# Sliding-window attention beside a SwiGLU: edge products on 64x32 and 32x64 tiles, V for sixteen heads, full products as column strips

## The chip, the core and the metric

The kernel runs on one core of one Trainium2 chip. The metric is the device time of one execution in microseconds, lower is better; the time before is the median of three runs, 240.3 us (240.14 to 240.38).

## What is computed

The input x has 2048 rows of 512. A 32-head attention (head size 16) with a causal window of 256 keys and a SwiGLU with 1376 hidden columns both read x; a sigmoid gate per row mixes their results.

```python
H = 32; Dh = D // H; W = 256
qkv = (x @ wqkv).reshape(B, S, 3, H, Dh)            # then q, k, v
scores = einsum("bhqd,bhkd->bhqk", q, k) * (Dh ** -0.5)
mask = (idx[:, None] - idx[None, :] >= 0) & (idx[:, None] - idx[None, :] < W)
p = softmax(where(mask, scores, -1e9))
a = (p @ v) @ wo
b = (silu(x @ w1) * (x @ w3)) @ w2
g = sigmoid((x * gate_w).sum(-1))
out = g * a + (1 - g) * b
```

Operands are bf16.

## The kernel before

**Tiles.** x is held transposed (xT, 512 channels in four chunks of 128 partitions, 2048 columns). The attention is done in four passes c = 0 to 3, each with the eight heads whose 128 channels fill the partitions: four row groups s of 32 partitions hold two heads each, a = 0 and 1. Keys are kept twice, once per head of the pair, with the other head's 16 partitions set to zero (`rowsA` is that 0/1 column), so that a score product of 32 rows serves one head. Queries stand in qT. The 2048 rows are 16 key tiles t of 128, or four stretches of 512 (tq for projections, h for edges, w for values).

**Scores.** `main_batch(c, t)` computes, for key tile t, the queries from 64 behind the tile's start, 256 of them (L560): eight matmuls of 32 rows x 128 columns, four row groups side by side, into the four banks of `su`. ScalarE takes the exponential of all of `su` at once (L564) into an Em buffer, and GpSimd cuts the two triangles outside the window (L569, L574). That leaves, for each key tile, two blocks of 64 x 64 in the window: the first 64 queries against the first 64 keys ("lo") and queries 320 to 383 against the last 64 keys ("hi"). `edge_batch(c, h)` makes these for four key tiles and both heads of each pair in one go (L610). Its stationary operand is 128 wide: 64 keys of one head and 64 of the other, side by side in `kz`; the result has one head's keys in partitions 0 to 63 and the other's in 64 to 127. The exponentials go to an Ee buffer (L614), masked by GpSimd (L627) and VectorE (L633, L637). The last key tile's queries 64 to 127 ride along in the last edge batch.

**Values.** `pv(c, w)` sums, for the 512 queries of stretch w, exponentials times V over the key tiles that reach them (L700). V has 16 columns per head and a column of ones (the softmax's denominator), so each matmul has 17 columns and is placed on one of four 32-column tiles; four heads stand side by side in a bank of `ch`, and the two heads of the pairs take two banks, jobs[0] and jobs[1]. For the edge blocks the stationary V has 128 rows, of which the other head's 64 are zero; these copies are made by GpSimd (L517) from the V that VectorE wrote (L512). VectorE then transposes, divides by the denominator and transposes back into OT (L724 to L734).

**The rest.** Projections of K and Q (L422), of V (L499, in pass 0 with the gate's weight as a 129th column), the up products (L825; the last 96 hidden columns are treated as 64 joint ones and 32 "tail columns", L785), the down products (L875), the output products (L905) with the mix and the DMA out (L909, L915). All of these are full products of 128 rows x 128 columns on TensorE.

**Order.** Nothing is looped at run time. Each piece is an `Op` with an engine, an assumed duration, a due time and buffers taken and freed; `Plan.emit` places the ops one by one on a list schedule and issues them in that order. The order on each engine is thus fixed when the program is built. `form` names an op's shape on TensorE ("full", "row", "column"); a change of form adds SWITCH to the plan, and `rank` groups ops of one form. The due times come from the numbers in K. `su` is one buffer of four banks, `ch` four buffers of one bank.

Of the kernel before, what the change touches and what calls it, by code (L numbers as in the profile page):

```python
# [26 lines left out]
class Op:  # L27
    __slots__ = ("eng", "dur", "lat", "fn", "deps", "due", "take", "free", "seq", "start", "end", "slots", "hold", "form")

    def __init__(self, eng, dur, fn, deps, due, take, free, lat, seq, form):  # L30
        self.eng, self.dur, self.fn, self.due, self.lat, self.seq = eng, dur, fn, due, lat, seq
        self.deps = [d for d in deps if d is not None]
        self.take, self.free = take, free
        self.start = self.end = None
        self.hold = 0.0
        self.form = form

# [8 lines left out]
class Plan:  # L46


    def __init__(self, slots, beside, apart):
        self.ops = []  # L50
        self.slots = slots
        self.beside, self.apart = beside, apart

# [16 lines left out]
    def rank(self, op, form):  # L70
        due = op.due
        if op.eng == "PE" and op.form != "full":
            if form != "full":
                due -= self.beside
            elif op.form == "column":
                due += self.apart
        return due, op.seq

    def emit(self):
# [15 lines left out]
        while ready:  # L95
# [23 lines left out]
            if eng == "PE" and op.form != form:  # L119
                est = max(est, engine.get(eng, 0.0) + SWITCH)  # L120
                form = op.form
# [20 lines left out]
        self.order = order  # L142
        for est, op in order:
            op.fn()
# [3 lines left out]
def kernel(  # L148
# [27 lines left out]
    NV = NT * 4  # L176
    LO, HI = NV, 2 * NV
    VW = DH + 1
    HALF = (0, 1, 2, 3, 4)
    SCALE = float(DH) ** -0.5  # L180
# [17 lines left out]
    wB = pp.tile([P, NDC, 2 * FB], BF16, name="wB")  # L198
# [3 lines left out]
    kz = pp.tile([P, NT, 4, KB], BF16, name="kz")  # L202
    qT = pp.tile([P, S + KB], BF16, name="qT")
    k1 = pp.tile([P, NT, 2, KB], BF16, name="k1")
    vs = pp.tile([P, 3 * NV, 2 * VW], BF16, name="vs")
    gwr = pp.tile([NDC, P], BF16, name="gwr")
    wv0 = pp.tile([P, NDC, P + 4], BF16, name="wv0")
# [8 lines left out]
    mlast = pp.tile([P, 2, KB], BF16, name="mlast")  # L216
    Em = [pp.tile([P, 4, 2, 256], BF16, name=f"Em_{i}") for i in range(9)]
    Ee = [pp.tile([P, 4, 4, 2, KB], BF16, name=f"Ee_{i}") for i in range(2)]
    kt = [pp.tile([P, 512], BF16, name=f"kt_{i}") for i in range(2)]
# [10 lines left out]
    K = {"T0": 6.663, "TA": 234.789, "TF0": -1.359, "TF1": 251.583, "PV": 0.213, "EDGE": -2.966, "HOLD": -4.301, "LEAD": 9.863, "QLEAD": -3.864, "V": 5.26, "O0": -0.819, "O1": 5.827, "O2": 6.852, "O3": 24.592, "FE": -3.084, "PE": -2.787, "VE": -3.291, "MK": 4.4, "UP": 2.598, "_km": 1.0, "_lo": 1.0, "LE": 4.467, "ADJ": 0.265, "SEP": 1.114, "BE": -2.825}  # L230
    plan = Plan({"su": 1, "ch": 4, "Em": len(Em), "Ee": len(Ee), "kt": 2, "tt": 2, "h1": 2,
# [3 lines left out]


    def half_of(base, a):
        return slice(0, KB) if (a == 1) == (base == LO) else slice(KB, P)
# [19 lines left out]
    def constants3():  # L258
        nc.gpsimd.memset(qT[:, S:S + KB], 0.0)
        for m in (medge, mlast):  # L260
            nc.gpsimd.memset(m[:], BIG)
        for m, k, sign, halves in ((medge, 0, 1, (0, KB)), (medge, 1, -1, (0, KB)),
                                   (mlast, 0, 1, (0, KB)), (mlast, 1, 1, (KB,))):
            for lo in halves:
                nc.gpsimd.affine_select(out=m[lo:lo + KB, k, :], in_=m[lo:lo + KB, k, :],
                                        pattern=[[sign, KB]], compare_op=ALU.is_ge, fill=0.0,
                                        base=0 if sign > 0 else -1, channel_multiplier=-sign)

    def constants4():
        nc.gpsimd.memset(hb[:], 0.0)  # L270
        nc.vector.memset(vs[:, LO:LO + NV, :], 0.0)
        nc.vector.memset(vs[:, HI:HI + NV, :], 0.0)
        nc.gpsimd.memset(vs[:, 0:NV, DH:2 * VW:VW], 1.0)
        for base in (LO, HI):
            for a in range(2):
                nc.gpsimd.memset(vs[half_of(base, a), base:base + NV, a * VW + DH], 1.0)

# [106 lines left out]
    def gw_out():  # L384
        nc.vector.tensor_copy(out=wv0[:, :, P:P + 1],
                              in_=ch[gjob.at["ch"]][:].bitcast(BF16)[:, 0:NDC].rearrange("p (c o) -> p c o", o=1))

    def wv0_copy():
        nc.vector.tensor_copy(out=wv0[:, :, 0:P], in_=wqkv_sb[:, :, 2 * D:2 * D + P])

    a = add("PE", 0.1, gw_turn, [gw_in], 9.407, take=[(gjob, "ch")])
    wv0_ready = [add("DVE", 0.15, gw_out, [a], 9.0, free=[(gjob, "ch")]),
                 add("DVE", 0.3, wv0_copy, [qkv_in[2]], 9.0)]
# [11 lines left out]
    def projections(c, tq):  # L405
# [3 lines left out]
        if c:  # L409
            war = [su_ops[(c - 1, t)] for t in range(4 * tq, 4 * tq + 4)]  # L410
            war.append(far_ops[(c - 1, tq)])
            vwar = [pv_ops[(c - 1, w)] for w in range(tq, min(NTC, tq + 2))]
            qwar = [su_ops[(c - 1, t)] for t in range(max(0, 4 * tq - 3), 4 * tq + 4)]
            qwar += [far_ops[(c - 1, h)] for h in range(max(0, tq - 1), tq + 1)]
        else:
            vwar, qwar = [], []
        src = list(xt_ready[tq]) + [qkv_in[2 if c < 2 else 3]]

        def chain(job, col, lo, hi, t0=0, t1=512):
            pst = ch[job.at["ch"]]  # L420
            for dc in range(lo, hi):
                nc.tensor.matmul(pst[:, t0:t1], lhsT=wqkv_sb[:, dc, col + c * P:col + (c + 1) * P],  # L422
# [10 lines left out]
        kv0 = kz[:, 4 * tq:4 * tq + 4, 1:3, :]  # L433
        kv1 = kz[:, 4 * tq:4 * tq + 4, 0:4:3, :]

        k1v = k1[:, 4 * tq:4 * tq + 4, :, :]

        def by_half(src):
            return src.rearrange("p (k h t) -> p k h t", h=2, t=KB)
        a = project(kj, D, [qkv_in[0 if c < 2 else 3]], due, [(kj, "ch")])  # L440
        if c == 0:
            def kev_a():
                nc.vector.tensor_scalar_mul(
                    out=kv0, in0=by_half(ch[kj.at["ch"]][:]),
                    scalar1=rowsA[:, 0:1])

            def kev_b():
                nc.scalar.activation(
                    out=k1v, in_=by_half(ch[kj.at["ch"]][:]),
                    func=ACT.Copy, scale=rowsA[:, 1:2])  # L450
            b = add("DVE", 0.69, kev_a, [a], due, free=[(kj, "ch")])
            def kev_c():
                nc.gpsimd.tensor_copy(out=kv1, in_=k1v)
            m = add("ACT", 0.69, kev_b, [b], due, free=[(kj, "ch")])
            k_ready[(c, tq)] = [b, m]
            ke_ready[(c, tq)] = [add("POOL", 0.62, kev_c, [m], due)]
        else:
            def kev():
                nc.vector.tensor_copy(out=kt[kj.at["kt"]][:], in_=ch[kj.at["ch"]][:])

            def kcopy():
                (nc.vector if K["_km"] else nc.gpsimd).tensor_copy(out=kv1, in_=k1v)

            def kmask(h):
                (nc.vector if K["_km"] else nc.gpsimd).tensor_scalar_mul(  # L465
                    out=(kv0, kv1, k1v)[h], in0=by_half(kt[kj.at["kt"]][:]),
                    scalar1=rowsA[:, min(h, 1):min(h, 1) + 1])
            b = add("DVE", 0.69, kev, [a], due, take=[(kj, "kt")], free=[(kj, "ch")])
            k_ready[(c, tq)] = [add("DVE" if K["_km"] else "POOL", 0.3 if K["_km"] else 1.64, lambda h=h: kmask(h), [b] + war, due, free=[(kj, "kt")])
                                for h in (0, 2)]  # L470
            ke_ready[(c, tq)] = [add("DVE" if K["_km"] else "POOL", 0.3 if K["_km"] else 0.62, kcopy, k_ready[(c, tq)], due)]
# [12 lines left out]

        vdue = due + K["V"]
        res = []
        gates = []
        for m0, nm in ([(4 * tq, 2), (4 * tq + 2, 2)] if c == 0 else [(4 * tq, 4)]):
            vj = Job()
            w = P + 1 if c == 0 else P  # L490

            def vmm(lo, hi, vj=vj, m0=m0, w=w):
                pst = ch[vj.at["ch"]]
                for mm in range(lo, hi):
                    m = m0 + mm
                    for dc in range(NDC):
                        rhs = (wv0[:, dc, 0:w] if c == 0
                               else wqkv_sb[:, dc, 2 * D + c * P:2 * D + (c + 1) * P])
                        nc.tensor.matmul(pst[:, mm * w:(mm + 1) * w], lhsT=xT[:, dc, m * P:(m + 1) * P],  # L499
                                         rhs=rhs, start=(dc == 0), stop=(dc == NDC - 1))  # L500

            def v_of(rows, base, a, m0=m0, nm=nm):
                return vs[rows, base + 4 * m0:base + 4 * (m0 + nm), a * VW:a * VW + DH]

            def v_all(vj=vj, m0=m0, nm=nm, w=w):
                out = vs[:, 4 * m0:4 * (m0 + nm), :].rearrange("p i (a e) -> p i a e", a=2)[:, :, :, 0:DH]
                src = ch[vj.at["ch"]][:, 0:nm * w].rearrange("p (m w) -> p m w", w=w)[:, :, 0:P]
                src = src.rearrange("p m (s a d) -> p m s a d", s=4, a=2)
                out = out.rearrange("p (m s) a d -> p m s a d", s=4)
                for m in range(1 if w == P else nm):  # L510
                    n = nm if w == P else 1
                    nc.vector.tensor_copy(out=out[:, m:m + n], in_=src[:, m:m + n])  # L512

            def v_half(base, a, v_of=v_of):
                to = half_of(base, a)
                half = slice(0, KB) if base == LO else slice(KB, P)
                nc.gpsimd.tensor_copy(out=v_of(to, base, a), in_=v_of(half, 0, a))  # L517

            def zact(vj=vj, m0=m0, nm=nm, w=w):
                z = ch[vj.at["ch"]][:, 0:nm * w].rearrange("p (m w) -> p m w", w=w)  # L520
# [448 lines left out]
```

## Time and profile before

| | |
|---|---|
| median of three runs | 240.3 us |
| the profiled execution, its time / its span | 240.56 / 238.8 us |
| granted TensorE clock | 1.00 |
| first projection starts / last matmul ends | 5.84 / 235.7 us into the span |
| TensorE, mean duration of a 512-column full product (L825) | 380 ns, x320 |
| main scores (L560), 480 matmuls | 278 and 268 ns |
| edge scores (L610), 512 matmuls | 189 ns |
| value products reading Ee (L700), 992 matmuls | 193 ns |
| ScalarE, exponential of 128 x 2048 (L564, L614) | 1877 ns, x76 |
| GpSimd, V copies of L517 | 30.6 us busy in 80 |
| VectorE, V out of PSUM (L512) / key copies (L462) / last edge mask (L637) | 8.2 + 3.7 / 4.8 / 5.4 us busy |
| VectorE, mix and bank out (L909) | 737 ns, x15 |

Each figure is from one execution. "Busy" is the union of an engine's instructions. Matmuls overlap each other: a duration of 380 ns does not mean that the next one starts 380 ns later, so the timeline's start times say what one costs. In the timeline a row is a group of equal neighbours: start, time from the first start to the last end, engine, line, operation, out<-in, rows*columns of the stationary operand, moving operand, count. In the list of waits each row says who waited for whom, the total, how many times and the longest. In the list of stretches each engine's busy time stands with its count of instructions, in the order TensorE, its weight loads, VectorE, ScalarE, GpSimd.

### The profile page before, as it was taken

Reading aid. Unit: us, or ns where it says so; the run is one execution under the profiler, and the core shown is the slowest. Engines: PE = TensorE matmul, PEld = TensorE weight load, DVE = VectorE, ACT = ScalarE, POOL = GpSimd, SP = SyncE. Lnnn points to the kernel's source line nnn. Section 1 sums busy time; section 2 is a strip of 40 time slices with the busy share of each in tenths; the row PEclk is TensorE's granted clock in tenths of the full one; section 3 lists DMA queues with packets and bytes.
Section 4 is the critical chain, followed back from the end, with each engine's and each line's share of the span. In section 5 each row is a group of like instructions: output and inputs, shape, how many; then the busy total and the mean of one; then the engine's idle time right before and its main releaser. Section 6 shows DMA issues by size and latency. Waiting matters only on the chain.

```text
span 238.8 us, 8528 instructions
## 1 busy us (share of the span) xinstructions
PE 231.3 (97%) x3738; PEld 118.8 (50%) x3738; DVE 201.3 (84%) x342; ACT 171.2 (72%) x141; POOL 159.6 (67%) x261
## 2 busy tenths in 40 slices
PE   8999999999999999999989899999999999999994
PEld 8554544546463543545454544545454545445442
DVE  5576998967699989996699999987899897969885
ACT  3389798876867898666858788776768989766510
POOL 7259967979857877587475777768494968575500
PEclk9999999999999999999999999999999999999999
DMA  7999980000000000000000000000000001002133
GB/s 199 205 335 276 201 212 17 5 1 3 3 3 0 5 11 11 7 0 3 3 3 3 1 8 20 3 0 3 3 3 5 3 0 25 3 22 69 52 108 110
DMA packets 20413, 11.59 MB, mean 49 GB/s; under 512 B 9656, under 2 KB 20376, under 8 KB 20376
## 3 DMA queue, kind: packets, MB, share of 16 engines
q1 hardware_dynamic: 19680, 10.59, 17.7%
q8 instruction: 29, 0.48, 0.9%
q10 hardware_dynamic: 696, 0.46, 0.6%
q14 instruction: 8, 0.07, 0.1%
HBM read 6.85 MB, written 2.10 MB: 37 GB/s over the span
## 4 chain that ended last, share of the span: by engine, by line
PE 72%; DVE 19%; ACT 4%; issue 2%; POOL 1%; DVEq 0%; ACTq 0%
PE ch L825 20%; PE ch L875 15%; PE ch L422 9%; PE ch L700 8%; PE su L560 6%; PE ch L905 5%; PE ch L499 4%; ACT Ee L614 4%; DVE h L839 3%; PE su L610 2%; DVE Ee L633 2%; DVE hT L845 2%; DVE Ee L637 2%; DVE tn L724 2%; DVE k L465 2%
## 5 line engine op out<-in xcount | busy, mean ns | idle before, releaser
L564 ACT ACTIVATE Em<-su 128x2048 bf16<-128x2048 f32 x60 | 112.6, 1877 | 34.6 <-PE su L560 31.4
L825 PE MATMUL ch<-xT,w_sb 128*128 128x512 bf16 x320 | 79.3, 380 | 0.5 <-DVE vs L512 0.3
L569 POOL TENSOR_SCALAR_AFFINE_SELECT Em<-Em 64x512 bf16<-64x512 bf16 x60 | 41.1, 685 | 32.5 <-ACT Em L564 26.9
L627 POOL TENSOR_SCALAR_AFFINE_SELECT Ee<-Ee 64x1024 bf16<-64x1024 bf16 x32 | 42.7, 1333 | 21.4 <-ACT Ee L614 19.3
L825 PEld LDWEIGHTS <-w_sb 128*128 128x128 bf16 x320 | 28.4, 98 | 34.8 <-issue 6.9
L875 PE MATMUL ch<-w_sb,hT 128*128 128x512 bf16 x160 | 40.3, 380 | 0.0
L574 POOL TENSOR_SCALAR_AFFINE_SELECT Em<-Em 64x512 bf16<-64x512 bf16 x56 | 37.3, 665 | 3.2
L614 ACT ACTIVATE Ee<-su 128x2048 bf16<-128x2048 f32 x16 | 30.0, 1876 | 10.3 <-PE su L610 7.6
L422 PE MATMUL ch<-xT,wqkv_sb 128*128 128x512 bf16 (+1 forms) x136 | 34.3, 372 | 0.0
L517 POOL COPY vs<-vs 64x256 bf16<-64x256 bf16 (+1 forms) x80 | 30.6, 382 | 5.1 <-DVE vs L512 1.8
L839 DVE SCALAR_TENSOR_TENSOR h<-tt,ch 128x512 bf16<-128x512 bf16 (+1 forms) x44 | 29.6, 677 | 4.7 <-ACT tt L835 4.5
L845 DVE SCALAR_TENSOR_TENSOR hT<-h,ch 128x512 bf16<-128x512 bf16 x40 | 27.1, 677 | 1.9
L835 ACT ACTIVATE tt<-ch 128x512 bf16<-128x512 f32 (+1 forms) x44 | 25.7, 594 | 2.4 <-PE ch L825 2.2
L700 PEld LDWEIGHTS <-vs 128*17 128x17 bf16 x1664 | 21.1, 92 | 8.6 <-issue 6.3
L700 PE MATMUL ch<-Em,vs 128*17 128x256 bf16 (+2 forms) x672 | 22.9, 242 | 2.4 <-DVE h L839 1.7
L700 PE MATMUL ch<-Ee,vs 128*17 128x64 bf16 x992 | 22.6, 193 | 0.0
L875 PEld LDWEIGHTS <-hT 128*128 128x128 bf16 x160 | 13.9, 98 | 16.8 <-issue 3.2
L422 PEld LDWEIGHTS <-wqkv_sb 128*128 128x128 bf16 x136 | 12.4, 99 | 12.7 <-issue 2.1
L499 PEld LDWEIGHTS <-xT 128*128 128x128 bf16 x256 | 15.8, 97 | 5.6 <-issue 1.8
L880 DVE TENSOR_SCALAR bsb<-ch,omg 128x512 bf16<-128x512 f32 x15 | 11.2, 747 | 7.6 <-PE ch L875 7.4
L560 PE MATMUL su<-qT,kz 32*128 32x256 bf16 x240 | 17.3, 278 | 0.2
L560 PE MATMUL su<-qT,k 32*128 32x256 bf16 x240 | 16.7, 268 | 0.0
(81 smaller groups left out, 257.4 us busy)
## 6 DMA issues: line engine op xcount, KB each, us to landing
out_dram<-ot SPq DMA_DIRECT2D x15, 128.0 KB, 1.7
wqkv_sb<-in_A_wqkv_dram SPq DMA_DIRECT2D x5, 256.0 KB, 5.7
w_sb<-in_B_w_dram SPq DMA_DIRECT2D x1, 1280.0 KB, 6.7
w_sb<-in_B_w_dram SPq DMA_DIRECT2D x2, 608.0 KB, 7.8
w_sb<-in_B_w_dram SPq DMA_DIRECT2D x2, 512.0 KB, 5.2
w_sb<-in_B_w_dram SPq DMA_DIRECT2D x2, 256.0 KB, 4.9
wo_sb<-in_A_wo_dram SPq DMA_DIRECT2D x1, 512.0 KB, 5.5
xs<-in_A_x_dram SPq DMA_DIRECT2D x1, 256.0 KB, 2.9
```

The lines of the kernel that those rows point to most:

```text
L422: nc.tensor.matmul(pst[:, t0:t1], lhsT=wqkv_sb[:, dc, col + c * P:col + (c + 1) * P], rhs=xT[:, dc, tq * 512 + t0:tq * 512 + t1], start=(d ...
L560: nc.tensor.matmul(su[:, s, a * 256:(a + 1) * 256], lhsT=head_keys(r, t, a), rhs=qT[r, q0:q0 + 256], start=True, stop=True)
L564: nc.scalar.activation(out=Em[job.at["Em"]][:], in_=su[:].rearrange("p s (a q) -> p s a q", a=2), func=ACT.Exp, scale=SCALE)
L569: nc.gpsimd.affine_select(out=e, in_=e, pattern=[[0, 8], [1, KB]], compare_op=ALU.is_ge, fill=0.0, base=0, channel_multiplier=-1)
L574: nc.gpsimd.affine_select(out=e, in_=e, pattern=[[0, 8], [-1, KB]], compare_op=ALU.is_ge, fill=0.0, base=-1, channel_multiplier=1)
L614: nc.scalar.activation(out=Ee[ej.at["Ee"]][:].rearrange("p s t k q -> p s (t k q)"), in_=su[:], func=ACT.Exp, scale=SCALE)
L627: nc.gpsimd.affine_select(out=e, in_=e, pattern=[[0, 4], [0, 4], [1, KB]], compare_op=ALU.is_ge, fill=0.0, base=0, channel_multiplier=-1)
L700: nc.tensor.matmul(po[32 * s:32 * s + VW, lo - 512 * w:hi - 512 * w], lhsT=vs[:, i, a * VW:(a + 1) * VW], rhs=mov, start=(n == 0), stop=(n ...
L825: nc.tensor.matmul(ch[job.at["ch"]][:], lhsT=wA[:, dc, :] if joint else w[:, dc, f * P:(f + 1) * P], rhs=xT[:, dc, tcb * 512:(tcb + 1) * 512],
L839: nc.vector.scalar_tensor_tensor(out=h1[job.at["h1"]][ru, :], in0=tt[job.at["tt"]][rg, :], scalar=1.0, in1=ch[job.at["ch"]][rg, :], op0=AL ...
L845: nc.vector.scalar_tensor_tensor(out=dst, in0=h1[job.at["h1"]][ru, :], scalar=0.5, in1=ch[up.at["ch"]][ru, :], op0=ALU.mult, op1=ALU.mult)
L875: nc.tensor.matmul(bps[:], lhsT=ht[:, mm * P:(mm + 1) * P], rhs=w2_sb[0:fs, f, :], start=(f == 0), stop=(f == NFC - 1))
```

## The change

- **Edge scores** take keys of one head at a time: 64 keys as a 32 x 64 stationary operand, the two heads of a pair on the two 64-column halves. `kz` and `k1` become one `kh` (both heads, keys in order), so the copies between them go.
- **Value edges** take 64 rows: head a's keys are partitions 64a to 64a + 63 of Ee, and V's 64 rows come from `vs` itself or, where the other half of the tile's keys is meant, from `vx`, a copy of V with its halves exchanged (one GpSimd copy for each half of two key tiles). The zeroed copies of V go. In `pv` the main products of both heads come first, then one op of form "half" with all edge blocks, in which a and s run innermost.
- **The last key tile** gets its queries 64 to 127 from the score batch of tile 14: that batch's 256 columns are 192 of tile 14 and 64 of tile 15, as two matmuls for each head; a second GpSimd select cuts tile 15's triangle. `mlast` goes.
- **V** is projected for sixteen heads (256 columns) at once in passes 0 and 2, and serves two passes. The gate's column moves from V's product to that of the tail columns (65 instead of 64 columns).
- **Strips.** Full products go through `product`. Where an unbroken run of full and column ops on TensorE holds a column op, all full products of the run are written as four matmuls of 32 columns each. The plan no longer counts a change between "full" and "column".
- The numbers in K are others, so due times and with them the order on all engines differ.

```diff
+        run = []
+        for op in [op for est, op in order if op.eng == "PE"] + [None]:
+            if op and op.form in ("full", "column"):
+                run.append(op)
+                continue
+            column = any(o.form == "column" for o in run)
+            for o in run:
+                o.strips = column
+            run = []
         for est, op in order:
+            self.strips = op.strips
             op.fn()
...
+    def product(out, lhsT, rhs, start, stop):
+        if not plan.strips:
+            nc.tensor.matmul(out, lhsT=lhsT, rhs=rhs, start=start, stop=stop)
+            return
+        for j in range(0, P, 32):
+            nc.tensor.matmul(out[j:j + 32], lhsT=lhsT[:, j:j + 32], rhs=rhs, start=start, stop=stop)
...
+                        product(pst[:, mm * 256:(mm + 1) * 256], lhsT=xT[:, dc, m * P:(m + 1) * P],
+                                         rhs=wqkv_sb[:, dc, 2 * D + cp * 256:2 * D + cp * 256 + 256],
+                                         start=(dc == 0), stop=(dc == NDC - 1))
...
+            def vcross(a, m0=m0):
+                to, at_ = slice(KB * a, KB * a + KB), slice(KB - KB * a, P - KB * a)
+                nc.gpsimd.tensor_copy(out=vx[to, m0:m0 + 2, :, 0:DH], in_=vs[at_, cp, m0:m0 + 2, a:16:2, 0:DH])
...
-                    nc.tensor.matmul(su[:, s, a * 256:(a + 1) * 256], lhsT=head_keys(r, t, a),
-                                     rhs=qT[r, q0:q0 + 256], start=True, stop=True)
+                    n = min(256, S - q0)
+                    nc.tensor.matmul(su[:, s, a * 256:a * 256 + n], lhsT=kh[r, a, P * t:P * t + P],
+                                     rhs=qT[r, q0:q0 + n], start=True, stop=True)
+                    if t == NT - 2:
+                        nc.tensor.matmul(su[:, s, a * 256 + n:(a + 1) * 256], lhsT=kh[r, a, P * t + P:P * t + 2 * P],
+                                         rhs=qT[r, S - KB:S], start=True, stop=True)
...
+                    for a in range(2):
+                        for s in range(4):
+                            r = slice(32 * s, 32 * s + 32)
+                            if q0 < S:
+                                nc.tensor.matmul(su[KB * a:KB * a + KB, s, (2 * i + k) * KB:(2 * i + k + 1) * KB],
+                                                 lhsT=kh[r, a, k0:k0 + KB], rhs=qT[r, q0:q0 + KB],
+                                                 start=True, stop=True)
...
+        def edges(last):
+            for n, (t, q, k) in enumerate(lows + highs):
+                for a in range(2):
+                    rows = slice(KB * a, KB * a + KB)
+                    for s in range(4):
+                        values = (vs[rows, c // 2, t, 8 * (c % 2) + 2 * s + a, :] if a == k
+                                  else vx[rows, t, 4 * (c % 2) + s, :])
+                        value(a, s, values, Ee[ejob[(c, "e", t // 4)].at["Ee"]][rows, s, t % 4, k, :], q - q0,
+                                last and n == len(lows + highs) - 1)
...
         for a in range(2):
-            prev = add("PE", streams(0, cut), lambda a=a: mm(a, 0, cut), deps + [prev], due, take=[(jobs[a], "ch")], free=frees,
-                       form="column")
-            ends.append(prev)
+            prev = add("PE", streams(early), lambda a=a: mains(a, early), mdeps + [prev], due, take=[(jobs[a], "ch")],
+                       free=mfree, form="column")
+        prev = add("PE", 0.25, lambda: edges(not final), edeps + [prev], due,
+                   free=[(ejob[(c, "e", h)], "Ee") for h in range(max(0, w - 1), w + 1)], form="half")
```

More of the change, by code (lines that the diff above doesn't have):

```diff
@@ L473, in projections @@
+            k_ready[(c, tq)] = [add("DVE" if K["_km"] else "POOL", 0.3 if K["_km"] else 1.64, lambda h=h: kmask(h),
+                                    [b] + war, due, free=[(kj, "ot")]) for h in range(2)]
         qj = Job()
@@ L505, in v_all @@
[L505 to L512, printed above, removed]
@@ L704, in streams, with value @@
-        def streams(n0, n1):
-            return 0.035 + sum(hi - lo for kind, t, lo, hi in todo[n0:n1]) / 2400
-        cut = len(todo) - 1 if final else len(todo)
-        ends = []
+        begun = set()
+        def value(a, s, values, e, col, last):
+            first = (a, s) not in begun
+            begun.add((a, s))
+            nc.tensor.matmul(ch[jobs[a].at["ch"]][32 * s:32 * s + VW, col:col + e.shape[-1]], lhsT=values, rhs=e,
+                             start=first, stop=last, skip_group_check=True)
```

302 lines of the change are left out of this document (104 added, 198 removed).

## The prediction

> **What bounds the kernel now.** I read the busy shares first, then who TensorE waited for, then its instructions in order of time, and last groups by shape and busy time by stretch. The page's first line, and TensorE's waits:
>
> ```profile
> PE 231.3 (97%) x3738; PEld 118.8 (50%) x3738; DVE 201.3 (84%) x342; ACT 171.2 (72%) x141; POOL 159.6 (67%) x261
> ...
> PE ch L700 <- DVE h L839: 1.7, 2, 0.9
> PE su L296 <- DVE warm L299: 1.1, 1, 1.1
> PE ch L700 <- DVE hT L845: 0.5, 1, 0.5
> PE ch L825 <- DVE vs L512: 0.3, 1, 0.3
> ```
>
> TensorE is busy for 97% of the span and its waits come to some 4 us, mostly of value products (L700) for a bank that VectorE has not yet emptied. So TensorE's own work sets the time, and what a matmul costs is not its duration (they overlap) but the distance to the next start. The timeline gives these distances:
>
> ```profile
> 104.61 0.29 PE L560 MATMUL su<-qT,kz 32*128 32x256 bf16 x4
> 104.73 0.28 PE L560 MATMUL su<-qT,k 32*128 32x256 bf16 x4
> 104.94 1.04 PE L875 MATMUL ch<-w_sb,hT 128*128 128x512 bf16 x4
> 105.81 0.38 PE L875 MATMUL ch<-w_sb,hX 96*128 96x512 bf16 x1
> 106.03 1.06 PE L499 MATMUL ch<-wqkv_sb,xT 128*128 128x128 bf16 x16
> 106.93 0.59 PE L875 MATMUL ch<-w_sb,hT 128*128 128x512 bf16 x2
> ...
> 107.78 1.04 PE L875 MATMUL ch<-w_sb,hT 128*128 128x512 bf16 x4
> 108.75 0.21 PE L700 MATMUL ch<-Em,vs 128*17 128x64 bf16 x4
> ...
> 109.37 0.20 PE L700 MATMUL ch<-Em,vs 128*17 128x64 bf16 x4
> 109.40 0.20 PE L700 MATMUL ch<-Ee,vs 128*17 128x64 bf16 x4
> 109.43 0.20 PE L700 MATMUL ch<-Em,vs 128*17 128x64 bf16 x4
> ```
>
> A full product of 512 columns takes 0.217 us (104.94 to 105.81 for four), one of 128 takes 0.056 (106.03 to 106.93 for sixteen). Four value products on four 32-column tiles start within 0.01 us of each other and the next four follow after 0.03 us: 64 columns cost the same 0.029 us for four as for one. Four scores of 256 columns on four 32-row tiles take 0.11 to 0.12. A change of tile shape adds to that: 104.73 to 104.94 is 0.21 where the stream is 0.11, and 107.78 to 108.75 is 0.97 where four products are 0.87. I take 0.093 us, the middle of all such places in the trace (full to row 0.312 less 0.216, row to full 0.200 less 0.110, full to column 0.309 less 0.216).
>
> By these distances the order before holds 206.1 us of streams and 170 shape changes behind the opening, 15.8 us. The opening (first projection at 5.84) and 4.3 us of waits in 13 places bring that to 232.0 of the 235.7 us up to the last matmul's end; most of what is left is some 0.01 us that a first product after a wait or a change takes extra.
>
> **The change, part by part.** All counts are of instructions in the two programs' orders.
>
> *Value edges.* Before, 992 products of 64 columns read Ee (L700), four at a time: 248 x 0.029 = 7.2 us. After, 960 of 64 rows x 32 columns, ordered so that eight in a row lie on eight different tiles and two banks. If eight overlap as four do now, 120 x 0.029 = 3.5 us; if only four, 7.0. The trace holds no 64-row tile. I take the eight: L610 shows four row tiles side by side and L700 four column tiles, each starting 2 to 4 ns after the last, so eight need some 25 of the 29 ns. Another 32 products of 64 columns move to Em (key tile 15): 8 x 0.029 = 0.2. Sum -3.5 us (lower bound of the gain 0).
>
> *Edge scores.* 512 of 32 rows x 128 columns (128 groups x 0.029 = 3.7 us) become 960 of 32 x 64: 3.5 us with eight tiles, 7.0 with four. I take -0.2, worst +3.3.
>
> *Score tile 14.* Its eight 256-column scores become eight pairs, 192 columns and then 64 on the same row tile, pair by pair. All 3738 matmuls of the trace start in program order, and a second group on the same row tiles waits until the first has streamed (104.61 to 104.73). So each 64 waits for its 192 (0.083 us by 54 such groups of L700, 0.074 plus three starts) and the next pair waits behind it: 8 x 0.086 = 0.7 us, where eight scores took 0.22. Four such batches: +1.9 us. Were the pairs of other row tiles free to pass, it would be 0. I take the first, since nothing in the trace passes. The 32 edge scores that key tile 15 no longer needs are in the counts above. [...]
>
> *V.* 256 products of 128 or 129 columns (0.056 to 0.058: 14.4 us) become 128 of 256 (0.109, as L422's and L905's of that width): 14.0. -0.4 us. The gate's column moves to the tail columns: 64 products of 65 instead of 64 columns, 0.03 us. One shift in time: V now comes in c 0 and 2 alone.
>
> *Strips.* 596 instructions of 128 rows x 32 columns (532 of 512 columns, 64 of 256), four to a product, stand for 149 full products. Four 256-column value products on column tiles start 0.110 after the four before, against 0.109 for one full product, so a strip product costs what the full one does, +0.15 us for all. What strips buy are shape changes: written full, the new order would have 195, as it is 171, against 172 before. So strips only pay for the new shapes, and the sum of changes is -0.1 us. Bounds: 0 to, if strips overlapped badly, 0.01 a product more, 1.5 us.
>
> *Other engines.* VectorE loses L462 (4.8 us), L637 (5.4), the two memsets (1.9), 0.13 on each of twelve key masks (1.5) and 0.9 of V copies: some 14 of 201 us. GpSimd loses 30.6 us of L517 for 32 copies at 0.425 (13.6), and gains four selects at 0.69: -16 us net with L453. ScalarE loses four small tanh. None is on the path by itself; what they can move is TensorE's waits:
>
> ```profile
> 90.00:120.00 30.00, 29.45 (x490) 14.59 (x489) 25.61 (x41) 22.11 (x16) 19.96 (x29) 1.00 0.02 5
> 120.00:150.00 30.00, 28.24 (x507) 14.70 (x507) 29.08 (x45) 23.35 (x20) 21.24 (x31) 1.00 0.03 7
> ```
>
> The fourth figure behind the stretch is VectorE: 29.08 of 30 us in 120 to 150, the start of c = 2, where most of the waits are (0.96 us at 120, 0.83 at 135, 0.19 and 0.07 near 149). There V copies double (+2.7 us in that c) against -3.5 of other work, so I leave these waits. In c = 1 and 3 VectorE loses some 6 us each; the waits at 72 to 73 (0.55), 94 (0.62) and 184 (0.16) go: -1.2 us, bounds 0 and -4.3 (no wait left).
>
> *The end.* After the last value products TensorE had 8.8 us of output and up/down products, now 10.4; VectorE has five steps of the last normalisation and 13 evictions in it, at 0.62 from start to start 10.3 us. It keeps pace just about; the last eviction and its transfer (3.2 us behind the last matmul) stay.
>
> *Sum.* -3.5 - 0.2 + 1.9 - 0.4 + 0.2 - 0.1 - 1.2 = -3.3 us. The profiled execution took 240.56 us around its span of 238.8, the median of the runs is 240.3. 240.3 - 3.3 = **237.0 us**.
>
> **Rivals.**
>
> *Eight tiles do not overlap (12%, slower).* Value edges and edge scores each run four at a time. Price 3.5 + 3.5 us: 237.0 + 7.0 = 244.0 us; if only one of the two suffers, 240.5. For it: no such shape in the trace, and sixteen instructions would have to issue in 29 ns where eight do now. Against: bursts at the start of L610 and L700 issue one every 1.5 to 2 ns. It turns into a loss as soon as a group of eight takes over 0.043 us (3.3 / 240 more than 0.029).
>
> *Weight loads set the pace of small tiles (10%).* Four loads of 17 columns go by in 29 ns at L700. Were that their limit, an edge score group with two loads of 64 columns per row tile, 128 in place of 68, takes up to 0.055 us: 120 x 0.026 = 3.1 us more, 240.1 us, no change; strips, 128 columns in up to 0.055, stay hidden under 0.217. Against: the first group after a change is late by 0.006 us at 17 columns and by 0.010 with full loads, so loads look short and parallel. [...]
>
> *Tile 14's pairs pass each other (16%, faster).* Then 1.9 us less: 235.1 us.
>
> *VectorE falls behind at c = 2 (8%).* Twice the V copies meet the stretch that is 97% full. If its 2.7 us of extra copies all become waits of L700's banks, and the -1.2 of elsewhere stays: 239.7 us; if the -1.2 fails too, 240.9. Against: its total there falls. Half of this counts as faster, half as slower.
>
> **How the numbers follow.** Forecast 54%, pairs pass 16%, loads 10%, no overlap 12%, VectorE 8%. 0.2% is 0.5 us, about what a measurement can tell here: faster means below 239.8, slower above 240.8. Faster: 54 + 16 + 4 = 74%. Same: 8 of the loads' 10. Slower: 12 + 4 + 2 = 18%. Alone, the forecast has 235.5 to 238.5 (waits gone, strips 1.5 dearer). The range takes in the passing pairs with a microsecond of waits gone below, 234.0, and loads and VectorE above, 241.0; the 244 stays outside.
>
> **What would show it.** Groups of eight edge products starting 0.03 us apart (0.06 would be the first rival, 0.05 on the scores alone the second). Score tile 14 as a batch of 0.7 us. Strip products 0.22 us apart with no gap between strips and value products. About 171 gaps of 0.09. VectorE near 187 us, GpSimd near 144, TensorE waits near 3 us, most of them in c = 2. I am wrong if TensorE's waits grow past 6 us, or if its work shrinks by 4 or more or not at all.

## The result, and the profile after

The changed kernel takes 242.45 us (median of 6 runs, 241.72 to 243.25) where the kernel before takes 240.22 (6 runs on the same chip, 239.69 to 240.38): ratio 1.0095, 95% interval 1.0068 to 1.0122. It is slower by 2.2 us; 237.0 was forecast.

The profiled execution took 241.72 us around a span of 240.0; the one before had 240.56 around 238.8. So the two traces show 1.2 us of the 2.2. The rest lies in the spread of the changed kernel's runs (1.5 us, against 0.7), which no profile here explains.

The page's first line after, then the waits of TensorE, then busy time by stretch (columns as before):

```profile
PE 234.2 (98%) x4537; PEld 122.9 (51%) x4537; DVE 183.2 (76%) x311; ACT 171.1 (71%) x137; POOL 146.2 (61%) x205
```

```profile
PE su L301 <- DVE warm L304: 1.1, 1, 1.1
PE ch L606 <- issue: 0.5, 1, 0.5
PE ch L247 <- DVE h L781: 0.4, 1, 0.4
```

```profile
90.00:120.00 30.00, 30.00 (x680) 15.74 (x677) 22.93 (x37) 22.40 (x16) 19.70 (x27) 1.00 0.03 6
120.00:150.00 30.00, 29.87 (x567) 16.55 (x566) 26.25 (x48) 23.21 (x21) 19.99 (x28) 1.00 0.03 7
```

VectorE and GpSimd lost about what was forecast (183 and 146 us, where 187 and 144 were expected), and the waits behind the opening fell further than forecast, from 4.3 us to 1.4 (by the gaps between starts; the list leaves out the small ones). TensorE is busy for all of 90 to 120. Yet the last matmul starts at 236.02 us, where it started at 235.38. TensorE got *slower at its own work*, and a busy share can't show that. The timeline can. One window's value edges (start, time from the first start to the last end, and at the end of the row the count of products):

```profile
105.71 1.06 PE L606 MATMUL ch<-Em,vs 128*17 128x64 bf16 x48
...
106.70 0.20 PE L606 MATMUL ch<-Ee,vs 64*17 64x64 bf16 x4
106.71 0.20 PE L606 MATMUL ch<-Ee,vx 64*17 64x64 bf16 x4
...
106.80 0.33 PE L606 MATMUL ch<-Ee,vx 64*17 64x64 bf16 x8
106.95 0.22 PE L606 MATMUL ch<-Ee,vs 64*17 64x64 bf16 x4
106.99 0.22 PE L606 MATMUL ch<-Ee,vx 64*17 64x64 bf16 x4
107.02 0.22 PE L606 MATMUL ch<-Ee,vs 64*17 64x64 bf16 x4
...
107.15 0.22 PE L606 MATMUL ch<-Ee,vs 64*17 64x64 bf16 x4
107.30 0.29 PE L510 MATMUL su<-qT,kh 32*128 32x256 bf16 x4
```

At first four products start every 0.015 us, so eight in 0.03, as forecast: eight tiles do run side by side. The entry of eight products at 106.80 holds a pause; behind it four take 0.033 us, 8.3 ns for each product with its weight load. By the single starts, the pause comes behind the 32nd product, here and in each of the 32 batches of edge products (16 of values, 16 of scores); it is 99 to 108 ns long in 31 of them and 90 in one. A batch of 64 edge scores goes the same way: 32 in 0.139 us, a pause of 0.099, then 0.067 for each eight. It takes 0.497 us from first start to last, where the 32 products of 128 columns took 0.22 before. The granted clock is 1.00 in both kernels from 90 to 120 us, so the clock is not the cause.

The `issue` line in the list of waits is something else, one stop in one of the 16 value windows:

```profile
200.89 0.20 PE L606 MATMUL ch<-Ee,vs 64*17 64x64 bf16 x2
201.58 0.20 PE L606 MATMUL ch<-Ee,vs 64*17 64x64 bf16 x2 [0.48 <-issue]
```

From start to start it is 0.68 us, and the profile shows nothing that was waited for. Two kernels below with the same value edges (half the edge scores, no strips) don't have it there. So it is no part of what the new shapes cost, and its cause stays open.

Start to start, summed over all matmuls (the distances between full groups in the kernel before are taken as what a product needs, and the rest is counted as excess):

| term | forecast, us | traces, us |
|---|---|---|
| value edges, with the 32 products that moved to Em | -3.5 | 7.3 to 8.0, and 0.2: +1.0 (0.7 of it is the stop at 200.89) |
| edge scores | -0.2 | 3.75 to 7.6: +3.8 |
| score tile 14 | +1.9 | 0.22 to 0.23 a batch: 0 |
| V | -0.4 | -0.4 |
| waits | -1.2 | -2.9 to -4.0 |
| changes of shape, strips, the rest (what remains of the sum) | +0.1 | -0.9 to +0.2 |
| up to the last matmul's start | -3.3 | +0.6 |
| behind it | 0 | 3.46 to 3.99: +0.5 |

The waits have two values: 4.3 to 1.4 us counts as the prediction does; a distance less that of the same two products elsewhere without a wait gives 5.0 to 1.0. The row below them changes with it.

### The profile page after: what moved, and what is told of

It is laid out like the page before. It is cut to its first block, busy times and chain, and to the rows that moved or that the text cites. A ratio compares the mean times of both kernels' runs of the same rounds, so it can differ in the third digit from the quotient of the medians.

```text
span 240.0 us, 10034 instructions
## 1 busy us (share of the span) xinstructions
PE 234.2 (98%) x4537; PEld 122.9 (51%) x4537; DVE 183.2 (76%) x311; ACT 171.1 (71%) x137; POOL 146.2 (61%) x205
## 4 chain that ended last, share of the span: by engine, by line
PE 90%; POOL 3%; DVE 2%; issue 2%; ACT 2%; DMA 1%; DVEq 0%; POOLq 0%
PE ch L247 55%; PE ch L250 12%; PE ch L606 9%; PE su L510 8%; PE su L562 4%; ACT Em L517 2%; PE su L301 1%; POOL Ee L572 1%; DMA out_dram<-ot 1%; POOL Em L522 1%; PE ch L364 1%; DVE ot L851 1%; POOL Em L527 1%; DVE nt L660 0%; DVE xs L654 0%
## 5 line engine op out<-in xcount | busy, mean ns | idle before, releaser
L247 PE MATMUL ch<-xT,w_sb 128*128 128x512 bf16 x295 | 72.6, 380 | 0.4 <-DVE h L781 0.4
L522 POOL TENSOR_SCALAR_AFFINE_SELECT Em<-Em 64x512 bf16<-64x512 bf16 x64 | 45.1, 707 | 40.3 <-ACT Em L517 38.2
L527 POOL TENSOR_SCALAR_AFFINE_SELECT Em<-Em 64x512 bf16<-64x512 bf16 x56 | 38.2, 682 | 3.4
L247 PE MATMUL ch<-w_sb,hT 128*128 128x512 bf16 x128 | 31.3, 380 | 0.0
L247 PE MATMUL ch<-xT,wqkv_sb 128*128 128x512 bf16 (+1 forms) x115 | 29.0, 365 | 0.0
L606 PEld LDWEIGHTS <-vs 128*17 128x17 bf16 (+1 forms) x1184 | 21.6, 88 | 7.4 <-issue 2.1
L510 PE MATMUL su<-qT,kh 32*128 32x256 bf16 (+1 forms) x480 | 23.8, 271 | 0.1
L492 POOL COPY vx<-vs 64x256 bf16<-64x256 bf16 x32 | 12.8, 400 | 9.0 <-DVE vs L484 7.7
L577 DVE TENSOR_TENSOR Ee<-Ee,medge 128x1024 bf16<-128x1024 bf16 (+1 forms) x16 | 12.9, 804 | 6.3 <-ACT Ee L567 6.0
L510 PEld LDWEIGHTS <-kh 32*128 32x128 bf16 x480 | 7.6, 92 | 19.1 <-issue 17.1
L606 PE MATMUL ch<-Em,vs 128*17 128x192 bf16 (+2 forms) x704 | 16.4, 239 | 0.0
```

The source lines that it names most:

```text
L247: nc.tensor.matmul(out, lhsT=lhsT, rhs=rhs, start=start, stop=stop)
L510: nc.tensor.matmul(su[:, s, a * 256:a * 256 + n], lhsT=kh[r, a, P * t:P * t + P], rhs=qT[r, q0:q0 + n], start=True, stop=True)
L522: nc.gpsimd.affine_select(out=e, in_=e, pattern=[[0, 8], [1, KB]], compare_op=ALU.is_ge, fill=0.0, base=0, channel_multiplier=-1)
L527: nc.gpsimd.affine_select(out=e, in_=e, pattern=[[0, 8], [-1, KB]], compare_op=ALU.is_ge, fill=0.0, base=-1, channel_multiplier=1)
L606: nc.tensor.matmul(ch[jobs[a].at["ch"]][32 * s:32 * s + VW, col:col + e.shape[-1]], lhsT=values, rhs=e, start=first, stop=last, skip_group ...
```

## The experiments

Two theories stood for the slow batches. **Feed**: the count of instructions sets the pace. 64 of them, 32 products with their loads, are at hand and go faster than 8.3 ns a product; behind them come a pause of 0.10 us and then the pace at which instructions come. The figures are those of the changed kernel's trace above; that instructions are held at hand (one expectation says queue) and come at a pace of their own is the theory, and no trace here shows it. **Tiles**: eight tiles can't hold the fast pace, whatever the count.

**Half the edge scores.** With the k = 1 blocks (those of the far edge) left out a batch has 32 products.

```diff
-                            if q0 < S:
+                            if q0 < S and k == 0:
```

> Leaves out half of each edge score batch (the blocks of the far edge, k = 1), so each batch has 32 matmuls instead of 64 (48 in the last of a pass); the output is not the reference's. Theory F (instruction feed): a run of load and matmul pairs is fast for 32 pairs, that is 64 instructions, then pauses for 0.1 us and goes on at 8.3 ns a pair. Then every batch is 0.14 us from first to last start, with no pause, instead of 0.50 (0.36 for 48): 12 x 0.357 + 4 x 0.224 = 5.2 us less, 237.3 us from 242.45. Theory T (eight tiles side by side cannot hold their pace, whatever the number of instructions): the work halves, 32 x 8.3 ns = 0.27 us a batch, 3.7 us less, 238.7 us.

Measured 236.69 us (235.75 to 237.58), ratio to before 0.9842 (0.9812 to 0.9872). In its timeline the whole batch, from its start at 110.84 to the next product, takes 0.26 us with the change of shape:

```profile
110.84 0.33 PE L562 MATMUL su<-qT,kh 32*64 32x64 bf16 x32
111.10 0.61 PE L250 MATMUL ch<-w_sb,hT 128*32 128x512 bf16 x8
```

Every batch goes by in 0.139 us from first start to last, without a pause. Half the products cost 28% of the time (0.139 of 0.497), for the same eight tiles. By tiles a half would cost a half.

**Twice the columns.** Each edge score streams 128 columns instead of 64, into places that the next one overwrites; the count of instructions stays.

```diff
-                                nc.tensor.matmul(su[KB * a:KB * a + KB, s, (2 * i + k) * KB:(2 * i + k + 1) * KB],
-                                                 lhsT=kh[r, a, k0:k0 + KB], rhs=qT[r, q0:q0 + KB],
+                                o0, q1 = min(2 * i + k, 6) * KB, min(q0, S - P)
+                                nc.tensor.matmul(su[KB * a:KB * a + KB, s, o0:o0 + P],
+                                                 lhsT=kh[r, a, k0:k0 + KB], rhs=qT[r, q1:q1 + P],
```

> Each edge score matmul streams 128 columns instead of 64, same number of instructions; the scores are overwritten by their neighbours, so the output is not the reference's. Theory F: eight pairs then need 0.056 us to stream, 7 ns a pair, close to the 8.3 at which instructions come, so a batch of 64 stays at 0.45 to 0.50 us and the kernel at 242.4 us, within 0.5. Theory T: twice the columns take twice the time, 1.0 us a batch, 16 x 0.45 = 7 us more, 249 us.

Measured 242.15 us (241.66 to 242.90), ratio 1.0085 (1.0059 to 1.0110): twice the stream at the same time as the changed kernel. Its batch of 48 products and, for comparison, that of the changed kernel:

```profile
113.49 0.63 PE L563 MATMUL su<-qT,kh 32*64 32x128 bf16 x48
114.05 1.05 PE L250 MATMUL ch<-w_sb,hT 128*32 128x512 bf16 x16
```

```profile
112.96 0.57 PE L562 MATMUL su<-qT,kh 32*64 32x64 bf16 x48
113.46 0.40 PE L250 MATMUL ch<-w_sb,hT 128*32 128x512 bf16 x4
```

0.56 against 0.50 us. The first 32 products take 0.215 now (0.139 in the changed kernel), since they stream twice as much; then it is 8.7 ns a product. The pause gets shorter: 0.56 less 0.215, fifteen steps of 8.7 ns and the 0.14 that the changed kernel's batches have up to the next product leaves less than 0.08 us for it, by this estimate.

**The kernel before, with every edge score product twice.** This is the test without a new shape: 64 products of 32 rows x 128 columns, on four tiles only.

```diff
+                    for s in range(4):
+                        r = slice(32 * s, 32 * s + 32)
...
+                        nc.tensor.matmul(su[:, s, (2 * i + k) * KB:(2 * i + k + 1) * KB], lhsT=keys,
+                                         rhs=qT[r, qs:qs + KB], start=True, stop=True)
```

> The kernel before with every edge score product written twice, 64 pairs of 32 x 128 in a batch instead of 32; the result is the same. Theory F: the limit is the instructions, not the small tiles: 32 pairs at 7 ns as now, then 8.3 ns a pair, 0.49 us in all and 16 x 0.27 = 4.3 us more, 244.5 us. If the limit belongs to eight tiles side by side, four row tiles keep 7.3 ns a pair to the end: 0.46 us, 3.8 us more; the distance between starts behind the 32nd pair tells.

Measured 244.50 us (244.48 to 244.51), ratio 1.018 (1.0133 to 1.0227), so the time tells nothing, as the two expectations lie 0.5 apart. The timeline does:

```profile
20.27 0.21 PE L610 MATMUL su<-qT,kz 32*128 32x64 bf16 x4
20.30 0.20 PE L618 MATMUL su<-qT,kz 32*128 32x64 bf16 x4
...
20.59 0.22 PE L618 MATMUL su<-qT,kz 32*128 32x64 bf16 x4
20.63 0.22 PE L610 MATMUL su<-qT,kz 32*128 32x64 bf16 x4
20.66 0.22 PE L618 MATMUL su<-qT,kz 32*128 32x64 bf16 x4
20.70 0.22 PE L610 MATMUL su<-qT,kz 32*128 32x64 bf16 x4
20.73 0.22 PE L618 MATMUL su<-qT,kz 32*128 32x64 bf16 x4
```

Four old products start every 0.029 us for the first 32 (0.224 us in all), and 0.033 apart near the end: 8.3 ns a product, the same figure as in the new shapes, with other rows, columns and tiles. What they share is one load and one matmul each, 4.17 ns an instruction if both count alike. No run here has a load that serves several products, so whether loads, products or both are counted is not shown. That it is not the time since the run began that counts is seen in the trace of before: 0.6 us into a value run, behind products with longer streams, five groups of four (109.345 to 109.490) still follow each other by 0.029 us, 7.3 ns a product.

**The value edges in two runs.** The near blocks go ahead of the main value products, the far ones behind, at most 32 products a run; the op that takes both banks needed an edit of the plan as well.

```diff
-        prev = None
+        prev = add("PE", 0.13, lambda: edges(lows, False), edeps, due, take=[(jobs[0], "ch"), (jobs[1], "ch")], form="half")
         for a in range(2):
...
-        prev = add("PE", 0.25, lambda: edges(not final), edeps + [prev], due,
+        prev = add("PE", 0.13, lambda: edges(highs, not final), edeps + [prev], due,
```

> The value edges of a stretch in two ops, 32 near blocks before the main value products and 16 or 32 far blocks behind them, one change of shape more for each stretch. Theory F: neither run has more than 32 pairs, both go at 3.6 ns a pair without a pause; a stretch costs 0.115 + 0.115 + 0.1 for the change instead of 0.48 (0.115 + 0.06 + 0.1 instead of 0.35 in the first of a pass): 12 x 0.15 + 4 x 0.07 = 2.1 us less, 240.3 us, if the order's waits stay. Theory T: the pace stays at 8.3 ns a pair and the changes come on top, 1.6 us more, 244 us.

Measured 243.06 us (242.30 to 243.66), ratio 1.0118 (1.0091 to 1.0145): a miss in the time, a hit in the stage. No run has the pause of 0.1 us, most go by in 0.115 us, and their excess falls from 4.5 to 1.1 us (0.85 of what is left is two waits inside runs). But the plan found another order, with 200 changes of shape instead of 171 and 2.7 us of waits instead of 1.4.

**The same with the plan held.** So that nothing is ordered anew, the near blocks were written between the main products of the two banks by the op that was there.

```diff
-            prev = add("PE", streams(early), lambda a=a: mains(a, early), mdeps + [prev], due, take=[(jobs[a], "ch")],
+            prev = add("PE", streams(early), lambda a=a: (a and edges(lows, False), mains(a, early)), mdeps + [prev], due, take=[(jobs[a], "ch")],
...
-        prev = add("PE", 0.25, lambda: edges(not final), edeps + [prev], due,
+        prev = add("PE", 0.25, lambda: edges(highs, not final), edeps + [prev], due,
```

The plan doesn't know of this, so in some windows the first run reads near blocks that GpSimd has not masked yet.

> The changed kernel with its value edges written in two runs of at most 32 products each, the first of them between the main products of the two banks, and nothing else moved: plan, other engines and waits as they were. Theory of the instruction feed (fast for 32 load and product pairs at hand, then 8.3 ns a pair): both runs go at about 0.115 us, the excess of the value edges falls from 4.5 to about 1.1 us, 32 further shape changes cost about 0.065 us each (2.1 us, as the 29 further ones of the kernel with the runs moved in the plan), net -1.3 us: 241.1 us, give or take 0.5. Theory that eight tiles cannot hold the pace: nothing is gained and the changes are paid, 244.5 us.

Measured 244.17 us (242.74 to 245.26), ratio 1.0163 (1.0128 to 1.0198), which is the number of the wrong theory. One window in its timeline:

```profile
105.82 0.61 PE L606 MATMUL ch<-Em,vs 128*17 128x64 bf16 x24
106.37 0.20 PE L606 MATMUL ch<-Ee,vs 64*17 64x64 bf16 x4
...
106.47 0.20 PE L606 MATMUL ch<-Ee,vx 64*17 64x64 bf16 x4
106.60 0.62 PE L606 MATMUL ch<-Em,vs 128*17 128x64 bf16 x24
107.16 0.20 PE L606 MATMUL ch<-Ee,vx 64*17 64x64 bf16 x4
...
107.26 0.20 PE L606 MATMUL ch<-Ee,vs 64*17 64x64 bf16 x4
107.39 0.29 PE L510 MATMUL su<-qT,kh 32*128 32x256 bf16 x4
```

Both runs are fast: 0.10 us from the first group of four to the last. The excess falls from 4.5 to 0.8 us, more than the feed theory asked; without stops and waits inside the runs, from 3.9 to 0.1. What the expectation had wrong is the price of a change: at the 16 into the first runs and the 16 out of them the next start comes 0.12 us behind the last one, 3.7 us more in all than products of a run need, where 0.065 each, 2.1 us, was expected. The distance is not longer than at the changes of before: there it was 0.126 us from the last value product to the first score. Waits for the exponential of the near blocks add 2.3 us, and 0.9 of other waits are gone; the last matmul starts 1.3 us later than in the changed kernel (the profiled execution, 242.74 us, is the fastest of the six). The time alone would have settled on the wrong theory.

**Edge scores of 128 columns again.** VectorE copies the 64 keys of both heads side by side (`ke`, two slots), and an edge score is one product of 32 rows x 128 columns, as before: at most 32 to a batch.

```diff
+        def ke_copy(a):
+            nc.vector.tensor_copy(out=ke[:, h % 2, :, a, :],
+                                  in_=kh[:, a, 512 * h:512 * h + 512].rearrange("p (k x) -> p k x", x=KB))
...
+                            nc.tensor.matmul(su[:, s, (2 * i + k) * KB:(2 * i + k + 1) * KB],
+                                             lhsT=ke[r, h % 2, 2 * i + k, :, :].rearrange("p a x -> p (a x)"),
+                                             rhs=qT[r, q0:q0 + KB], start=True, stop=True)
```

> The changed kernel, with the edge scores as 32 products of 32 rows x 128 columns again (both heads' 64 keys side by side, from a copy that VectorE makes: 32 copies of 512 columns, some 0.35 us each), all else as changed but for one Em buffer less. Theory F: 32 pairs are what the queue holds, a batch is 0.22 us again instead of 0.50 (0.36) and the change behind it 0.02 shorter: 12 x 0.29 + 4 x 0.16 = 4.1 us less than 242.45, 238.3 us, below the kernel before. If the loss came from elsewhere, or if 11 us of VectorE copies and the missing buffer turn into waits, 241 us or more.

Measured 238.41 us (10 runs, 237.93 to 239.61), ratio to before 0.9929 (0.9909 to 0.9948). It computes all of the reference's output and is faster than both kernels. Its profile has lost some matmul records, but none in this batch, which took 0.50 us in the changed kernel:

```profile
112.63 0.35 PE L569 MATMUL su<-qT,ke 32*128 32x64 bf16 x24
112.92 0.40 PE L251 MATMUL ch<-w_sb,hT 128*32 128x512 bf16 x4
```

0.29 us. The price is 10 us more of VectorE work, and none of that is seen in the time: 4.0 us were won, 3.8 had gone into the edge scores.

**Both cures in one.** The values in two runs, by the plan, on this kernel.

> As scores128, and the value edges in two runs of at most 32 pairs around the main value products. Theory F: both kinds of edge run without a pause; 3.4 us less for value edges, 1.9 more for changes of shape around them: 1.5 us below scores128, 236.8 us, if the order's waits stay as they are; with as many more waits as split_values had, 238 to 239 us.

The two edits above (for the values, that of the first test) taken together measured 245.16 us (244.24 to 246.64), ratio 1.0220 (1.0162 to 1.0277), a miss by 6 us or more. Some lines of TensorE's waits:

```profile
PE ch L248 <- DVE h L788: 1.7, 3, 1.0
...
PE ch L251 <- DVE h L788: 1.0, 2, 0.8
PE ch L613 <- DVE qT L463: 0.8, 1, 0.8
PE ch L613 <- POOL Ee L579: 0.8, 1, 0.8
```

The near blocks are wanted earlier, before GpSimd has cut them, and behind that the order is another one, with 200 changes.

Then with the plan held, and the same unmasked blocks:

> The same edit on the changed kernel with edge scores of 128 columns (238.4 us). Feed: 237.1 us, give or take 0.5. Eight tiles as limit: 240.5 us.

Measured 241.92 us (241.39 to 243.16), ratio 1.0081 (1.0053 to 1.0110), 3.5 us slower than without. Again the excess of the value edges falls (3.8 to 0.6 us), and 32 changes and waits cost more than that.

**Tile 14 by groups.** All 192-column scores of a head are written first, then the four of 64.

```diff
                                      rhs=qT[r, q0:q0 + n], start=True, stop=True)
+                for s in range(4):
+                    r = slice(32 * s, 32 * s + 32)
                     if t == NT - 2:
```

> The changed kernel with tile 14's scores written group by group (four of 192 columns, then four of 64) instead of pair by pair. If matmuls on free row tiles pass a waiting one, as the trace of the changed kernel shows, nothing changes: a batch of 0.22 us and 242.4 us, within 0.4. If the order of the program held, 0.47 us less in each of four batches, 240.6 us.

Measured 242.05 us (10 runs, 240.63 to 243.44), ratio 1.0072 (1.0044 to 1.0101): no difference from the changed kernel that the intervals would show. The reason is in the changed kernel's own timeline, where its program lists 192, 64, 192, 64 and so on:

```profile
110.13 0.27 PE L510 MATMUL su<-qT,kh 32*128 32x192 bf16 x4
110.23 0.21 PE L513 MATMUL su<-qT,kh 32*128 32x64 bf16 x4
110.25 0.26 PE L510 MATMUL su<-qT,kh 32*128 32x192 bf16 x4
110.34 0.21 PE L513 MATMUL su<-qT,kh 32*128 32x64 bf16 x4
```

Four products of 192 start together, 6 to 7 ns apart, and the four of 64 come behind them. The second, third and fourth of the 192 have passed a 64 that stood ahead of them; each 64 starts 0.083 to 0.093 us behind the 192 on its own row tile, which is about what a group of 192 columns takes (0.083). The distances speak for the list having reached TensorE in that order: written group by group, in this run, the four of 192 start 3 to 4 ns apart.

**No strips.**

```diff
-                o.strips = column
+                o.strips = False
```

> All full products stay full (128 x 128), the order is the same. If a strip product costs what a full one does, 24 more changes of tile shape at 0.093 us come in: 2.2 us more, 244.7 us. If strips cost something by their four times as many instructions, the loss is smaller: at 0.01 us for each of the 149 products, 0.7 us more, 243.2 us; a gain would need over 0.015 us a product.

Measured 242.81 us (241.67 to 243.49), ratio 1.0105 (1.0072 to 1.0137). The order is the same, product by product, and has 195 changes instead of 171: start to start they cost 2.3 us more (0.093 us at each of the 18 from full products to value products, 0.106 at each of the 6 back), close to the 2.2 expected. But this profile has 0.8 us fewer waits and not the stop at 200.89, and the time differs from the changed kernel's by less than the intervals. So what the strips save in changes is seen, and what they bring to the time stays open; that they cost next to nothing themselves is seen in the changed kernel:

```profile
104.62 1.26 PE L250 MATMUL ch<-xT,wqkv_sb 128*32 128x512 bf16 x20
105.71 1.06 PE L606 MATMUL ch<-Em,vs 128*17 128x64 bf16 x48
```

Twenty strips, five products, take 1.09 us up to the first value product: 0.218 each, with no change between.

## Why the prediction was wrong

**The step that failed** is the cost of the edge products, "If eight overlap as four do now, 120 x 0.029 = 3.5 us". Eight do overlap, but only for 32 products (0.115 us in the values, 0.139 in the scores). The distance of 0.029 us was read off groups that stand in short runs. In the trace of before, the 112 products of a window take 1.34 us, 12 ns each, and its edge scores end at the 32nd; nothing there asked for more than 64 instructions at over one in 4.17 ns. The new batches ask for 48 or 64 pairs of a load and a matmul, of which the first 32 are fast. The upper bound of 7.0 us, by four tiles, lay near the 7.3 (without the stop) and 7.6 measured, but by counting tiles, so I gave it 12% on the evidence about tiles. Halving the batch, doubling the columns and doubling the old products show what sets the pace: how many short products with their loads stand in one run, not the tiles and not the columns. That it is the pace at which instructions come is the reading that fits all of these runs; no trace here shows the instructions coming, or where they would be held. The two terms are off by 4.5 (3.8 without the stop) and 4.0 us; tile 14 (1.9) and the waits with the rest (2.7) went better than forecast, which leaves the 3.9 us by which the last matmul's start was missed.

**The rivals.** "Eight tiles do not overlap" came out near in time and right in sign (244.0), by luck: its mechanism isn't there. I held against it that bursts issue one every 1.5 to 2 ns: the first 32 of a run are near that (3.7 ns a product in the values, 4.5 in the scores, two instructions each), but it is no measure of the pace behind them, 8.3 ns a product. "Weight loads set the pace of small tiles" fails as it was priced, by the columns that are loaded: loads of 17 columns in the values, of 64 in the scores and of 128 in the doubled old scores show the same 8.3 ns.

**Tile 14** was sized at +1.9 us on the premise "nothing in the trace passes". All starts of before are in program order, but by my reading of that program nothing in it had a reason to pass: no product that was ready stood behind one that was not. The rival "pairs pass each other" was right; its 1.9 us was simply lost among the 8.5 us that the two edge terms missed by. In all four batches of the changed kernel the four of 192 start within 0.02 us, ahead of three of 64 that are listed before them, and eight pairs take 0.22 to 0.23 us where 0.7 was forecast.

**V and the strip products** came out as worked out, at -0.4 us and at 0.216 to 0.218 us a product. The strips save 2.3 us of changes, as they were meant to, and the changes are the 171 that were counted.

**Waits** were right in sign and too small: -2.9 us or more instead of -1.2. I left the waits of c = 2 standing because VectorE was at 29.08 of 30 us there and V's copies double. It is at 26.25 now, and all but 0.3 us near 149 went with the rest.

**The end** was to stay and grew by 0.5 us: 3.46 us behind the last start became 3.99. In VectorE's timeline the last two evictions wait for an output buffer:

```profile
233.74 2.73 DVE L851 SCALAR_TENSOR_TENSOR ot<-ch,gq,bsb 128x512 bf16<-128x512 f32 x4 [0.61 <-PE ch L250]
236.66 0.88 DVE L851 SCALAR_TENSOR_TENSOR ot<-ch,gq,bsb 128x256 bf16<-128x256 f32 x2 [0.19 <-DMA out_dram<-ot]
```

I had the number of evictions (13 at 0.62 us) and said it keeps pace "just about". They take 0.66 us from start to start, 13 of them start behind the last values where 9 did before, and I priced the slack at nothing. The wait for the buffer is 0.19 of the 0.5 us; the rest is VectorE running behind.

## What to carry to other kernels

Ask how many instructions a stage issues in a row, not only how many tiles they cover: here a run of up to 32 small products went by in 0.14 us, and the next ones cost a pause of 0.1 us and 8.3 ns each, so one product with 128 stationary columns beat two with 64 (238.41 us against 242.45), even at the price of a copy on another engine that had time for it. TensorE's busy share can't show this (it rose to 98% while the kernel got slower); distances between starts inside a batch do. And when runs are split to stay short, each new change of tile shape at 0.12 us eats what the split brings.

## What the runs showed of the hardware

- In the 32 batches of edge products of the changed kernel (48 or 64 products, each with its own weight load) the first 32, which are 64 instructions, went at 3.7 ns a product in the values (4.3 in one) and 4.5 in the scores. Then came a pause of 90 to 108 ns, and behind it 8.3 to 8.4 ns a product but for eight single stops (0.034 to 0.035 us in six, 0.12 and 0.68). With twice the columns (wide_scores) it was 6.9 ns, a shorter pause, and 8.7 ns.
- In the old shape doubled (before_double, 64 products of 32 rows x 128 columns) four products started every 0.029 us at first, 7.3 ns a product, and every 0.033 near the end, 8.3 ns. So 8.3 ns a product, 4.17 ns an instruction if loads and matmuls count alike, was measured on 64 x 32, 32 x 64 and 32 x 128.
- Batches of 32 edge products showed no pause: 0.139 us (half_scores), 0.224 (before), and most of the value runs of split_values 0.115.
- Matmuls can start out of program order: in the changed kernel's score tile 14 four 192-column scores start 6 to 8 ns apart, and the four of 64 that are listed between them 0.064 to 0.073 us behind the last of these. In the kernel before all 3738 start in order.
- At a change between 64-column value products of 128 rows and of 64 rows the next start comes 0.12 us behind the last one (lowmid; 0.122 to 0.123 in the changed kernel), about as at the change from value products to scores in the kernel before (0.125 to 0.126).
